# Block-sparse attention and an MLP on one core: the weight loads are released at other points, and the order of all instructions is another one

## The chip, the cores and the metric

The kernel runs on one core of a Trainium2 chip. The metric is the device time of one execution, in microseconds (us). A time is the median of several executions; the profile is of one execution, taken by itself.

The engines are named as the profile names them: PE (TensorE, matmuls; PEld is its weight load), DVE (VectorE), ACT (ScalarE), POOL (GpSimd) and SP (SyncE, which here only issues DMAs). A queue of DMAs is filled by the engine that issues them: SP fills one, POOL another.

## The reference

```
# q, k, v: [4 batches, 8 heads, 768, 64]; w_in: [512, 2048]; w_out: [2048, 512]; all float32
k_rep = k.reshape(B, H, 12, 64, D).mean(axis=3)              # mean key of each block of 64
gate_scores = einsum('bhsd,bhnd->bhsn', q, k_rep)            # causal blocks only
top_idx = argsort(gate_scores)[..., -3:]                     # 3 best blocks of each query
mask = (own block or one of the 3) and (key not after query)
attn = softmax(where(mask, q @ k^T / 8, -1e9)) @ v
x = attn as 3072 tokens x 512
h = x @ w_in
g = 0.5 * h * (1 + tanh(sqrt(2/pi) * (h + 0.044715 h^3)))
out = g @ w_out                                              # [3072, 512] float32
```

## The kernel before

**Tiling.** The 32 heads are worked in 16 pairs (0 to 15), four pairs to a batch of 768 tokens. For a pair the kernel loads q, k and v, turns q and k so that the 64 dimensions of each head lie on partitions, forms the block means of k (`ks`) and their gate scores (the gate, PE), picks the blocks on DVE (`sel`: a transpose, ten rows of MAX8, comparisons), adds the mask through PE, takes the exp on ACT (`ats`), cuts the causal triangle on POOL (affine select), multiplies by v on PE, and normalises and turns the result into `xT`. Batch 0 (pairs 0 to 3) is done by `heads2` with turns on PE; later pairs by `heads`, with turns by DVE's stream transpose (L564) from pieces of 32 partitions in `sd` (four DMAs each for q and for k, L400).

After a batch's four pairs stands its MLP: `s1` (x @ w_in, L1122; gelu on ACT, L1134) and `s2` (the product with w_out). Batch 0 uses a plain second stage (`s2_plain`, L1322, of which f = 0 to 7 need the first half of w_out and f = 8 to 15 the second); batches 1 to 3 use a scheme with fewer products that needs sums of G and of w_out (L1309, L1291) and joins on DVE (L1421). Batch 3's first stage has fewer products too (`s1_seven`, L1211).

**Order.** Each piece of work is an operation that is added to a plan with its engines, what it depends on and which buffers it takes. It is not the program's text that sets the order: a list `ORDER` of operation numbers, with `BUFFER` (which buffer each takes) and `ENGINE` (for operations that may run on several engines, which one), is written out by hand at the top, and `Plan.run` emits the operations in that order. Costs and due times in the `add` calls served the search that made the list. Each engine works through its own instructions in the order in which they were emitted; an instruction that waits holds up what is behind it on that engine. PE also gets "warm" matmuls (L1524) on data of zeros, whose results nobody reads.

**Loads around the change.** Batch 0's q, k, v come through SP, and part of pair 0 through ACT's queue (L428), into room that G and TS need only later. `load_w` issues each weight as two halves from POOL (L460; w_in by columns, w_out by rows of the hidden dimension), and the DMA casts them to float16. In front of w_in stands a small POOL copy (L458) that reads a piece of v of pair 3, so that w_in starts after that v has landed; w_out follows w_in on POOL. `hold` (L1567) is a small DMA on SP that reads the last columns of w_in and so waits for its second half; behind it on SP stand k, q and v of pair 4, and so on. `fill` (L520) puts constant rows into kT. `cast_v` casts v on POOL.

Of the kernel before, what the change touches and what calls it, by code (L numbers as in the profile page):

```python
# [189 lines left out]
    "POOL": [  # L190
        586, 587, 646, 647, 707, 972, 973, 1035, 1036, 1097, 1098,
        1159, 1160, 1425, 1489, 1551, 1612]}


class Op:
# [1431 lines left out]
```

## Time and the profile before

| | us |
|---|---|
| median of 3 runs | 257.90 (257.89 to 257.94) |
| the profiled execution: its span | 256.0 |
| PE busy | 246.5 |
| DVE busy | 191.4 |
| ACT busy | 176.4 |
| POOL busy | 84.3 |
| first matmul with w_in, start | 38.45 |
| w_in issued, first half | 26.97 |
| w_out issued, first half | 34.74 |
| SP's hold lets go | 41.60 |
| last join on DVE, start | 252.70 |

The span is what the profiler's first and last instruction enclose; the time of a run is longer by some 1.9 us, which lie around it. In rows of the timeline the first two numbers are the start and the time of a group of instructions that follow each other on one engine; "x4" counts them, and a bracket gives idle time before them and what ended it. In rows of groups the numbers behind the bar are busy time and the mean of one instruction in nanoseconds.

### The profile page before, as it was taken

The page shows a single profiled execution, that of the slowest core. Times are in us where ns is not written, and L with a number is a line of the kernel's source. Part 1 is how long each engine was busy: PE and PEld are TensorE (multiplying, and loading weights), DVE is VectorE, ACT ScalarE, POOL GpSimd, SP SyncE. Part 2 cuts the span into 40 slices and gives each one's busy share as a digit, 9 for nine tenths or more (in the row PEclk, how much of TensorE's full clock was granted, in tenths as well). Part 3 has the DMA queues.
Part 4 walks back from the last instruction along what each step waited for, and adds up shares of the span by engine and source line. Part 5 has one row for each costly group of instructions (what it writes and reads, how often), then busy time and mean ns, then how long its engine had stood idle before and what let it go on. Part 6 is the DMA issues. An engine that isn't in the chain of part 4 may idle for free.

```text
span 256.0 us, 6451 instructions
## 1 busy us (share of the span) xinstructions
PE 246.5 (96%) x2485; PEld 171.2 (67%) x2485; DVE 191.4 (75%) x539; ACT 176.4 (69%) x225; POOL 84.3 (33%) x163
## 2 busy tenths in 40 slices
PE   7889999999998999999899999999999999999994
PEld 5667686555554566555578888555777786766883
DVE  2769751041989889989999999699889665579954
ACT  2399997634898998667969884566889957557300
POOL 8465970000239366223053853100056620000000
PEclk9999999999999999999999999999999999999999
DMA  8997599999989995999899699532112520040024
GB/s 164 218 208 166 94 212 191 213 161 157 184 142 165 153 143 99 172 179 199 127 174 110 144 188 166 118 94 69 26 34 72 64 74 1 3 165 0 3 82 164
DMA packets 130927, 32.62 MB, mean 127 GB/s; under 512 B 124528, under 2 KB 126928, under 8 KB 130896
## 3 DMA queue, kind: packets, MB, share of 16 engines
q1 hardware_dynamic: 126160, 27.62, 65.4%
q0 software_dynamic: 3136, 4.19, 9.7%
q10 hardware_dynamic: 1600, 0.39, 0.8%
q8 instruction: 19, 0.31, 0.5%
q14 instruction: 12, 0.10, 0.1%
HBM read 27.26 MB, written 6.29 MB: 131 GB/s over the span
## 4 chain that ended last, share of the span: by engine, by line
PE 51%; DVE 16%; SPq 11%; DMA 10%; POOL 4%; issue 3%; ACT 3%; ACTq 1%; DVEq 0%; POOLq 0%
PE bank L1372 17%; PE wide L1122 10%; SPq L400 9%; PE wide L1046 6%; PE wide L1211 5%; DMA w_in<-in_moe_w_in_dram 5%; PE bank L1085 5%; PE bank L1322 3%; DVE qT L367 3%; DMA sd<-in_k_dram 3%; DVE sel L719 2%; DVE s L564 2%; DVE XS L1309 2%; DMA G<-in_q_dram 2%; ACT ats L882 1%
## 5 line engine op out<-in xcount | busy, mean ns | idle before, releaser
L1122 PE MATMUL wide<-xT,w_in 128*128 128x384 f16 x416 | 72.6, 326 | 0.0
L1059 ACT ACTIVATE ats<-wide 128x896 f16<-128x896 f32 x72 | 63.4, 915 | 8.9 <-PE wide L1046 6.2
L1134 ACT ACTIVATE G<-wide 128x768 f16<-128x768 f32 x52 | 42.1, 810 | 27.3 <-PE wide L1122 27.0
L1122 PEld LDWEIGHTS <-w_in 128*128 128x128 f16 x416 | 40.0, 98 | 26.8 <-issue 1.3
L1073 POOL TENSOR_SCALAR_AFFINE_SELECT ats<-ats 128x256 f16<-128x256 f16 x72 | 33.3, 475 | 60.3 <-ACT ats L1059 60.2
L1046 PE MATMUL wide<-qT,kT 76*128 76x512 f16 (+3 forms) x192 | 39.1, 305 | 0.1
L564 DVE STREAM_TRANSPOSE s<-sd 128x768 f32<-128x768 f32 x24 | 23.1, 968 | 18.7 <-DMA sd<-in_k_dram 17.2
L1372 PE MATMUL bank<-w_out,G 128*128 128x256 f16 x216 | 31.4, 272 | 0.0
L1372 PEld LDWEIGHTS <-G 128*128 128x128 f16 x288 | 26.9, 98 | 6.0 <-issue 0.3
L1322 PE MATMUL bank<-w_out,G 128*128 128x512 f16 x96 | 28.1, 379 | 0.0
L365 POOL CAST kT<-s 64x768 f16<-64x768 f32 x17 | 15.2, 891 | 37.5 <-DVE s L564 37.0
L1421 DVE TENSOR_TENSOR osb<-bank,osb 128x512 f32<-128x512 f32 (+1 forms) x38 | 22.1, 592 | 5.1 <-PE bank L1372 4.5
L1085 PEld LDWEIGHTS <-ats 128*128 128x128 f16 x504 | 22.2, 98 | 3.9 <-POOL ats L1073 0.4
L1085 PE MATMUL bank<-v,ats 128*128 128x65 f16 x504 | 24.4, 194 | 0.2 <-POOL ats L1073 0.2
L1046 PEld LDWEIGHTS <-kT 76*128 76x128 f16 x192 | 17.3, 98 | 10.5 <-issue 0.8
L1372 PEld LDWEIGHTS <-XS 128*128 128x128 f16 x216 | 20.0, 98 | 5.5 <-DVE XS L1309 1.5
L1372 PE MATMUL bank<-TS,XS 128*128 128x256 f16 x144 | 22.0, 272 | 0.8 <-DVE XS L1309 0.7
L882 ACT ACTIVATE ats<-wide 128x1024 f16<-128x1024 f32 (+3 forms) x24 | 20.8, 924 | 1.3 <-PE wide L863 0.8
L365 POOL CAST v<-vsd 128x768 f16<-128x768 f32 x13 | 11.4, 875 | 13.8 <-DMA vsd<-in_v_dram 8.8
L969 DVE TENSOR_TENSOR xn<-bank,zr 128x384 f16<-128x384 f32 x24 | 13.4, 558 | 0.8
L719 DVE MAX8 sel<-sel 128x8 f32<-128x12 f32 x160 | 13.2, 158 | 0.6
L1322 PEld LDWEIGHTS <-G 128*128 128x128 f16 x96 | 8.9, 98 | 6.1 <-issue 0.3
(120 smaller groups left out, 358.6 us busy)
## 6 DMA issues: line engine op xcount, KB each, us to landing
out_dram<-osb SPq DMA_DIRECT2D x23, 256.0 KB
vsd<-in_v_dram SPq DMA_DIRECT2D x26, 192.0 KB
sd<-in_k_dram SPq DMA_DIRECT2D x48, 96.0 KB
sd<-in_q_dram SPq DMA_DIRECT2D x48, 96.0 KB
w_in<-in_moe_w_in_dram POOLq DMA_DIRECT2D x2, 1024.0 KB, 11.5
w_out<-in_moe_w_out_dram POOLq DMA_DIRECT2D x2, 1024.0 KB, 14.5
G<-in_k_dram SPq DMA_DIRECT2D x4, 192.0 KB
G<-in_q_dram SPq DMA_DIRECT2D x4, 192.0 KB
```

Source lines behind the costliest of these rows:

```text
L365: nc.gpsimd.tensor_copy(out=out, in_=in_)
L400: nc.sync.dma_start(out=T[key, p][64 * hh + 32 * a:64 * hh + 32 * a + 32], in_=SRC[key][b, 2 * hp + hh].rearrange("(t i) (a j) -> a i t j" ...
L564: nc.vector.transpose(out=T[key + "T32", p], in_=T[key, p].rearrange("p t j -> p (t j)"))
L882: nc.scalar.activation(out=T["at", u][:, :, 0:n], in_=plan.buf[("st",) + u].rearrange("p (h w) -> p h w", h=2)[:, :, 0:n], func=AF.Exp, bi ...
L1046: nc.tensor.matmul(st[:, x:e], kT16[i][h][0:76, s0:s0 + 128], qT16[i][h][0:76, s0 + (x - cb):s0 + (e - cb)], start=True, stop=True)
L1059: nc.scalar.activation(out=T["at", u][:, 0:n], in_=plan.buf[("st",) + u][:, 0:n], func=AF.Exp, bias=0.0, scale=SCALE)
L1073: nc.gpsimd.affine_select(out=dg, in_=dg, compare_op=ALU.is_ge, fill=0.0, base=0, pattern=[[0, 2], [1, 128]], channel_multiplier=-1)
L1085: nc.tensor.matmul(pvv[:, qc, 0:65], at[:, cb + (qc - jc) * 128: cb + (qc - jc + 1) * 128], v16[i][:, jc, h, :], start=(gi == 0 and jc == ...
L1122: nc.tensor.matmul(hps[:, 512 * e:512 * e + HALF], w_in16[:, ci, (2 * j + e) * 128: (2 * j + e + 1) * 128], T["xT", b][:, ci, HALF * h:HAL ...
L1134: nc.scalar.activation(out=G[:, :, h, j, :], in_=plan.buf["hps", b, j, h].rearrange("p (e w) -> p e w", e=2)[:, :, 0:HALF], func=AF.Gelu_a ...
L1322: nc.tensor.matmul(plan.buf["ops", b, ti], G[:, f % 2, 2 * ti // NC, f // 2, ti % (NC // 2) * 128:ti % (NC // 2) * 128 + 128], w_out16[:, ...
L1372: nc.tensor.matmul(dst[:, HD * h:HD * h + HD], FACT[m][0][:, j, t * 128:(t + 1) * 128], FACT[m][1][:, j, :], start=(clear and j == 0), sto ...
```

## The change

1. `load_w` now puts the waiting copy on POOL in front of both weights.
2. w_in waits for v of pair 2 (and, in the plan, for the issue of v of pair 3 on SP) in place of the landing of v of pair 3.
3. w_out is loaded after k and q of pair 4: its copy reads a piece of q of pair 4 and so waits until that has landed. The `hold` stays on SP ahead of k of pair 4.
4. `ORDER`, `BUFFER` and `ENGINE` are other lists. The matmuls are the same but for the warm ones, 63 in place of 39: 54 of them stand before the first product with w_in, formerly 24.

What follows from the new lists, read from the order on each engine:

- SP: a piece of q of pair 1 comes before k of pair 0, and batch 0's later pieces come in another order; behind the hold k, q of pair 4, then v of 4 with one piece of k of 7 between, k of 5, q of 5, then pieces of pairs 6 and 7 mixed.
- ACT issues the second half of q of pair 0 before the first.
- POOL: w_in stands after the first triangle select of pair 1, ahead of that pair's second select and of the casts of v of pairs 1 and 2; w_out stands after the fourth select of pair 3, ahead of the casts of k of pair 4 (both halves are POOL's now) and of v of pair 4.
- ACT has four casts and copies of q and k fewer between its first and its last exp of batch 0; DVE has them. Of later casts some go from DVE to ACT and some back; five casts of k (both of pair 4, one each of pairs 7, 12 and 15) go from DVE to POOL.
- PE: 96 of the 128 products of batch 0 with w_in come before the first product with w_out (72 before), and the gate of pair 4 does too. Between that and the first product that needs w_out's second half stand 22 products with w_in and 8 with w_out.
- The end: PE's last products are those of m7 of the second token group of batch 3, whose join is a whole row of 512, followed by a store of 256 KB; before, the end was a join of half a row and stores of 128 KB.

```diff
@@ lists at the top
 ORDER = [
...
 BUFFER = [
...
 ENGINE = {
...
@@ load_w
         def emit(_):
             x = const.tile([128, 16], FP32, name=f"after_{name}")[96:97]
-            if name == "in":
-                nc.gpsimd.tensor_copy(out=x, in_=T[after][96:97, 0, 1, 0:16])
+            src = T[after]
+            nc.gpsimd.tensor_copy(
+                out=x, in_=src[96:97, 0, 1, 0:16] if len(src.shape) == 4 else
+                src[96:97, 0, 0:16])
             for part in parts:
                 nc.gpsimd.dma_start(out=dst[part], in_=view[part])
@@ main loop
-    for x in ('in', 'out', ('k', HP + 0), ('q', HP + 0), ('v', HP + 0), ('k', HP + 1), ('q', HP + 1), ('v', HP + 1)):
+    for x in ('in', ('k', HP), ('q', HP), 'out', ('v', HP), ('k', HP + 1), ('q', HP + 1), ('v', HP + 1)):
         if x in weights:
             dst, src, parts, prio = weights[x]
             if not fills:
                 fills = [fill(i, chain) for i in range(NB)]
-            load_w(x, dst, src, parts, [ld[prev]] if x == "in" else
-                   [after_w["in", 0]], prio, prev)
+            load_w(x, dst, src, parts, [ld["v", 2], *chain] if x == "in"
+                   else [ld[prev], after_w["in", 0]], prio, ("v", 2) if x == "in" else prev)
             moved_w = [after_w[x]]
             chain += moved_w
```

More of the change, by code (lines that the diff above doesn't have):

```diff
@@ L21 @@
 ORDER = [
[134 rows of a table removed]
-BUFFER = [
[24 rows of a table removed]
[130 rows of a table added]
+BUFFER = [
[24 rows of a table added]
 ENGINE = {
     "ACT": [
[5 rows of a table removed]
[4 rows of a table added]
     "POOL": [
-        586, 587, 646, 647, 707, 972, 973, 1035, 1036, 1097, 1098,
-        1159, 1160, 1425, 1489, 1551, 1612]}
+        337, 338, 586, 587, 646, 647, 707, 708, 972, 973, 1035, 1036, 1097,
+        1098, 1159, 1160, 1425, 1426, 1489, 1551, 1612, 1613]}
 class Op:
```

321 rows, old and new, of tables (BUFFER, ENGINE, ORDER) are left out of this document.

## The prediction

> **What bounds the kernel now.** I read the page first (span, busy shares, slices, chain), then PE in windows, then the stretch from 12 to 66 us on each queue that the change touches.
>
> ```profile
> span 256.0 us, 6451 instructions
> PE 246.5 (96%) x2485; PEld 171.2 (67%) x2485; DVE 191.4 (75%) x539; ACT 176.4 (69%) x225; POOL 84.3 (33%) x163
> DMA  8997599999989995999899699532112520040024
> PE 51%; DVE 16%; SPq 11%; DMA 10%; POOL 4%; issue 3%; ACT 3%; ACTq 1%; DVEq 0%; POOLq 0%
> ```
> ```profile
> 0.00:38.40 38.40, 34.61 (x526) 1.00 1.00 177
> 38.40:50.30 11.90, 11.90 (x82) 1.00 1.28 201
> 66.00:102.00 36.00, 34.77 (x380) 1.00 0.97 141
> 102.00:138.00 36.00, 35.07 (x292) 1.00 1.18 169
> 138.00:256.00 118.00, 114.42 (x1120) 1.00 0.40 81
> ```
>
> The second view is PE by stage: length, busy time, matmuls, granted clock, DMA share, GB/s. PE is full almost everywhere; its idle time is 3.8 us before 38.4, 1.2 us from 66 to 102, 0.9 us from 102 to 138, and 3.6 us after, most of it the tail behind the last matmul. So the kernel is a line of matmuls, and a change gains or loses only where PE waits. The median, 257.9 us, lies 1.9 us above this execution's span; I sum against the span and add 1.9.
>
> Before 38.4 the pace is ACT's. Its rows from 12 us on, an exp, a cast, and the last exps:
>
> ```profile
> 12.50 1.03 ACT L882 ACTIVATE ats<-wide 128x1024 f16<-128x1024 f32 x1
> 13.42 0.49 ACT L363 COPY s<-bank 128x384 f32<-128x384 f32 x1
> 34.82 3.26 ACT L882 ACTIVATE ats<-wide 128x1024 f16<-128x1024 f32 x4 [0.43 <-POOL ats L908]
> L882 ACT ACTIVATE ats<-wide 128x1024 f16<-128x1024 f32 (+3 forms) x24 | 20.8, 924 | 1.3 <-PE wide L863 0.8 <-POOL ats L908 0.4
> ```
>
> The exps fill 20.8 of the 25.6 us from 12.50 to 38.08, and casts most of the rest. The weights come in beside this:
>
> ```profile
> 24.99 0.99 POOL L908 TENSOR_SCALAR_AFFINE_SELECT ats<-ats 128x512 f16<-128x512 f16 x2 [0.93 <-ACT ats L882]
> 25.94 0.83 POOL L365 CAST v<-TS 128x768 f16<-128x768 f32 x1
> 26.97 1.66 POOL L460 DMA_DIRECT2D w_in<-in_moe_w_in_dram  x2
> 34.74 1.78 POOL L460 DMA_DIRECT2D w_out<-in_moe_w_out_dram  x2
> ```
> ```profile
> L460 POOL DMA_DIRECT2D w_in<-in_moe_w_in_dram x2: 747/832/917, 27.0 to 27.9; - x2
> DMA to landing us min/median/max: 9.4/11.5/13.7
> ...
> L460 POOL DMA_DIRECT2D w_out<-in_moe_w_out_dram x2: 881/892/904, 34.7 to 35.6; - x2
> DMA to landing us min/median/max: 12.2/14.5/16.8
> ```
>
> So w_in's halves land 9.4 and 13.7 us after their issues, at 36.4 and 41.6; w_out's at 46.9 and 52.4. PE and SP around it:
>
> ```profile
> 38.45 1.79 PE L1122 MATMUL wide<-xT,w_in 128*128 128x384 f16 x10
> 40.24 10.24 PE L1122 MATMUL wide<-xT,w_in 128*128 128x384 f16 x62
> 50.31 0.38 PE L1322 MATMUL bank<-w_out,G 128*128 128x512 f16 x1
> 56.27 0.71 PE L1524 MATMUL bank<-XS 128*128 128x256 f16 x5
> 59.30 1.24 PE L1322 MATMUL bank<-w_out,G 128*128 128x512 f16 x5
> ```
> ```profile
> 41.60 0.58 SPq L1567 DMA_DIRECT2D after_in<-w_in  x1
> 42.22 7.13 SPq L400 DMA_DIRECT2D sd<-in_k_dram  x4
> 49.40 4.83 SPq L400 DMA_DIRECT2D sd<-in_q_dram  x4
> 55.43 3.07 SPq L400 DMA_DIRECT2D sd<-in_k_dram  x4
> 58.55 2.66 SPq L400 DMA_DIRECT2D sd<-in_q_dram  x4
> ```
>
> The first x@w_in matmul at 38.45 waits for neither weight. SP holds until w_in's second half is there (41.60); then k and q of pair 4 crawl beside w_out, 7.13 and 4.83 us for four pieces where later ones take 3.07 and 2.66.
>
> ```profile
> 54.40 0.98 DVE L564 STREAM_TRANSPOSE s<-sd 128x768 f32<-128x768 f32 x1 [14.96 <-DMA sd<-in_k_dram]
> 57.34 0.98 DVE L564 STREAM_TRANSPOSE s<-sd 128x768 f32<-128x768 f32 x1 [0.18 <-DMA sd<-in_q_dram]
> 63.94 0.35 DVE L703 STREAM_TRANSPOSE sel<-bank 128x160 f32<-128x160 f32 x1 [5.19 <-PE bank L687]
> PE bank L756 <- DVE madd L724: 2.1, 2, 1.2
> PE bank L1372 <- DVE XS L1309: 0.7, 1, 0.7
> ```
>
> DVE is idle for 15 us until k of pair 4, then for 5.2 us more; after that it is packed, and PE waits for it: 2.1 us at masks (the page's stalls near 81 and earlier) and 0.7 us at the sums of batch 1's second stage.
>
> **The change part by part.**
>
> *Start.* SP and ACT issue pair 0's and pair 1's first pieces in another order, with a piece of q of pair 1 ahead of k of pair 0. That should put the first exp about a microsecond later than 12.50. Against it, ACT issues four casts fewer between its first exp and its last (4 x 0.49 = 2.0 us); DVE makes them instead, ahead of the same exps. The exps themselves (20.8 us) do not change. I leave the end of the stretch where it was: 0, with 1.5 us either way. A gain here would also be eaten below, where PE waits for w_out, whose time does not hang on PE. Thirty more warm matmuls stand here. At 0.71 us for five they are 4.3 us of PE time, in a stretch where ACT decides; ACT's exps cover them, and if they did not, the cost would be up to that. After it there are six fewer, in waits that PE has anyway.
>
> *w_in.* Its issue now follows the first triangle select of pair 1 on POOL, one pair's v earlier, instead of the cast of v of pair 2. On ACT eight exps and two casts lead to it: 13.6 + 8 x 0.92 + 2 x 0.49 = 22.0, half of 0.99 for the select, and 1.4 for waits such as the exps' 1.3: 23.9. The bounds are 22.5, without waits, and 25, where before's selects stood. So w_in is issued 3 us earlier and has landed at 33.3 and 38.5. PE gains nothing by that: the first L1122 started 2 us after the first half had landed. Queued behind the wait on POOL are one select and the casts of v of pairs 1 and 2 (about 0.5 and 0.83 each); the two DMA issues (1.66) push them by under 2 us, and ACT's exps cover that. Without the cover it is 1.7 us at most.
>
> *k and q of pair 4, then w_out.* The hold on SP is over at 38.5, k is issued by 39.1 + 3.1 = 42.2 and q by 44.9, now with nothing beside them. Landing comes 2 to 3.1 us later (57.34 less the end of issue at 54.23 is 3.1): 46.9 to 48.0. POOL's copy waits for that piece, so w_out is issued at about 47.2, 12.5 us later than 34.74. Queued behind that wait on POOL are the casts of both halves of k of pair 4 and its v; they are wanted by scores that PE reaches about 15 us later, so they cost nothing here.
>
> The second half of w_out lands between 13.7 us (w_in's way, little beside it) and 16.8 us (its own, eight small pieces beside it) after 47.2: 61 to 64. I take 62, nearer the first, because pair 4's loads are out of the way; v of pair 4 and k of pair 5 are not. The first half lands at about 56.7 to 59.5, by 9.4 and 12.2.
>
> When does PE want them? Before, 72 matmuls with w_in (10 + 62) preceded the first with w_out; now 96 do. 24 more at 10.24 / 62 = 0.165 are 4.0 us, and with the gate of pair 4 now before it, PE stands at the first L1322 at 54.5. The first that needs the second half comes 22 matmuls with w_in and 8 with w_out later (22 x 0.165 + 8 x 0.22, from 1.24 for five): 59.9. Against 62 that is a wait of 2.1 us. Before, five warm matmuls stood in that place, 0.55 us (56.27 to 56.81). Net +1.5; from +0.5 (w_out at 61) to +3.5 (at 64).
>
> *Pairs 4 to 7.* Pair 4's transposes start about 10 us earlier on DVE, in its idle 14.96 us, and its gate comes before the first L1322. The masks of pairs 5 to 7 are still each a chain on DVE (transpose of the gate as in the row at 63.94, ten maxima, mask), and PE's order leaves about as much other work between a gate and its mask as before. Of the 2.1 us of mask waits I let 0.9 go, since PE also arrives later by the wait above; bounds 0 and 2.1. Net -0.9. Where DVE is not late here it is late at its next packed place, the sums below.
>
> *Batch 1's sums.* After the first stretch DVE carries about three copies fewer, moved to POOL and ACT; of the 0.7 us wait for XS I let 0.3 go (bounds 0 and 0.7).
>
> *The end.* Before, the last join is half a row and three 128 KB stores follow each other; now the last product is one of token 1, with a full-row join and a 256 KB store behind it:
>
> ```profile
> 252.70 0.42 DVE L1421 TENSOR_TENSOR osb<-bank,osb 128x256 f32<-128x256 f32 x1 [0.18 <-PE bank L1372]
> L1421 DVE TENSOR_TENSOR osb<-bank,osb 128x512 f32<-128x512 f32 x8 | 5.4, 689 | 1.4 <-PE bank L1372 1.2
> 251.41 2.08 SPq L1465 DMA_DIRECT2D out_dram<-osb  x3
> ```
>
> 0.69 - 0.42 = 0.27 for the join; for the store 0 to 0.5 (twice the bytes; 128 KB at the 201 GB/s of the second window is 0.65 us). I take +0.5 together.
>
> *Sum:* 0 + 1.5 - 0.9 - 0.3 + 0.5 = +0.8: a span of 256.8, and with 1.9 a time of 258.7.
>
> *A rule beside the row.* The Trainium skill, "DMA: Bandwidth & Descriptors", section "Anatomy of one DMA — SWDGE (gpsimd) path", gives 2.0 us plus the bytes over 436 GB/s for a transfer from this engine; as an estimate by that page both halves of w_out (2.1 MB) would be there 6.8 us after the issue. Here the trace differs: 13.7 us for the second half of w_in. By the rule w_out would be there at 54.0, PE would not wait for it, and the sum would be 257.2 or less, which is the first rival's side.
>
> **The rivals.**
>
> *Faster.* w_out comes in time. It needs the w_in issue at 22.5 and w_out in 13.7 us: then everything is 1.4 us earlier than I reckoned, and the second half lands at 47.2 - 1.4 + 13.7 = 59.5, before 59.9. PE loses nothing there, and the 0.55 of warm matmuls go; DVE, 10 us ahead with pair 4, lets the mask waits (2.1) fall to a half, and a wait of 0.7 at XS goes. 257.9 - 0.55 - 1.05 - 0.7 + 0.5 = 256.1, and 255.3 if the first stretch ends 0.8 sooner too. For it: DVE's 15 idle us and SP's 7.13. Against it: w_out 12 us later.
>
> *Slower still.* w_out competes with the small pieces of v of pair 4, k and q of pair 5, as it did with pair 4's, and takes 16.8 us or more. It decides from a landing after 62. Landing at 64 gives a wait of 4.1; nothing of the masks' time is won since pair 5's loads crawl too: 257.9 + 3.5 - 0.9 + 0.5 = 261.0.
>
> *Nothing happens.* The gap in the loads is only moved, from before w_in to before w_out, and PE's wait with it: +0.5 at w_out, -0.9 at masks, +0.4 at the end, 257.9. For it: the same matmuls in all but 24 warm ones; against it, that each of these three terms must fall at one end of its bounds.
>
> **How the numbers follow.** Forecast 0.37 (its own range 258.3 to 259.8); faster 0.33; slower still 0.17; nothing 0.13. The range holds all but about a fifth: 255.8, which leaves out the best ends of the first rival, to 261.0. About 0.5 us, 0.2%, is what a measurement of this kernel can tell from no change. Faster by more than that 0.34, within it 0.13, slower 0.53.
>
> **What would show it.** In the changed kernel: w_in issued near 23.9 and SP's hold over near 38.5; k and q of pair 4 in about 3 us each; w_out issued near 47; PE idle before an L1322 row between 54 and 62, released by DMA of w_out, some 2 us; mask waits at L756's counterpart of 1 to 1.5 us in place of 2.1; the last DVE row 0.69. It is wrong if the first x@w_in matmul moves by over a microsecond, if w_out lands within 12.5 us, or if PE waits for the masks as before or longer.

## The result, and the profile after

| | before | changed |
|---|---|---|
| median of 5 runs | 257.90 us (257.79 to 258.56) | 261.64 us (259.64 to 262.43) |
| ratio, 95% interval | | 1.013 (1.0105 to 1.0155) |
| the profiled execution: its time | | 262.43 us |
| its span | 256.0 | 260.7 |

The change makes the kernel slower by 1.3%. Slower was forecast, at 258.7 us; the median lies 2.9 us above that and 0.6 us above the range. The times of the changed kernel also spread over 2.8 us. Six more runs of it, beside an experiment below, gave a median of 260.13 us (259.38 to 261.59), ratio 1.0103 (1.0079 to 1.0128). In all eleven the times lie between 259.4 and 260.8, or between 261.6 and 262.4. The profile on this page is of the slowest of them; a second profile, of an execution of 259.95 us, is set beside it.

First the page of the changed kernel: span, busy times, the chain that ended last.

```profile
span 260.7 us, 6499 instructions
PE 250.5 (96%) x2509; PEld 174.1 (67%) x2509; DVE 193.4 (74%) x537; ACT 177.2 (68%) x222; POOL 88.2 (34%) x169
PE 66%; DMA 15%; DVE 8%; issue 3%; POOL 3%; ACT 2%; SPq 2%; ACTq 0%; POOLq 0%; DVEq 0%
```

PE is as full as before, and its share of the chain has gone from 51% to 66%. DVE fell from 16% to 8%, the SP queue from 11% to 2%, and DMA rose from 10% to 15%: what was late by DVE and SP now comes late by loads. The waits of PE say which (total, times, longest):

```profile
PE bank L1319 <- DMA w_out<-in_moe_w_out_dram: 2.0, 2, 1.4
PE bank L753 <- DVE madd L721: 1.9, 3, 1.0
PE bank L1369 <- DVE XS L1306: 0.2, 1, 0.2
```

The wait for w_out is new. The sums wait 0.2 us in place of 0.7. The masks wait 1.9 in place of 2.1, but these totals mix two places. In the kernel before, 0.90 us stand in the first stretch, ahead of pair 0's mask (at 9.71), and 1.20 later; in the changed kernel 0.96 and 0.54 stand in the first stretch, and only 0.39 later. The later masks, first before and then after the change:

```profile
81.74 0.45 PE L756 MATMUL bank<-ident,madd 128*128 128x128 f16 x5 [1.20 <-DVE madd L724]
```
```profile
96.18 0.45 PE L753 MATMUL bank<-ident,madd 128*128 128x128 f16 x5 [0.39 <-DVE madd L721]
```

The steps that led to the wait for w_out, on POOL, SP and PE of the changed kernel (start, time):

```profile
25.95 1.66 POOL L457 DMA_DIRECT2D w_in<-in_moe_w_in_dram  x2
...
48.93 0.20 POOL L453 COPY after_out<-sd 1x16 f32<-1x16 f32 x1 [7.81 <-DMA sd<-in_q_dram]
49.39 1.78 POOL L457 DMA_DIRECT2D w_out<-in_moe_w_out_dram  x2 [0.26 <-issue]
```
```profile
40.13 0.58 SPq L1564 DMA_DIRECT2D after_in<-w_in  x1
40.75 2.28 SPq L395 DMA_DIRECT2D sd<-in_k_dram  x4
43.07 2.54 SPq L395 DMA_DIRECT2D sd<-in_q_dram  x4
```
```profile
41.27 0.49 PE L1119 MATMUL wide<-xT,w_in 128*128 128x384 f16 x2
...
59.13 0.38 PE L1319 MATMUL bank<-w_out,G 128*128 128x512 f16 x1 [0.59 <-DMA w_out<-in_moe_w_out_dram]
...
65.96 0.38 PE L1319 MATMUL bank<-w_out,G 128*128 128x512 f16 x1 [1.37 <-DMA w_out<-in_moe_w_out_dram]
```

k and q of pair 4 take 2.3 and 2.5 us for four pieces, a little less than the 3.1 and 2.7 of the forecast. But the first product with w_in stands at 41.27 in place of 38.45, and w_in itself was issued only 1.0 us earlier than before. So the first stretch has lost 2.8 us by this mark, and w_out is issued at 49.39, 2.2 us after the time that was reckoned with.

The beginning shows where the two profiled executions part. PE's first rows of the profile above, and then of the second profile of the same kernel:

```profile
1.07 3.59 PE L1521 MATMUL bank<-XS 128*128 128x256 f16 x16 [1.07 <-DVE bmask L287]
5.39 0.88 PE L545 MATMUL bank<-identk,G 128*128 128x128 f32 x3 [0.72 <-DMA G<-in_q_dram]
6.05 1.49 PE L1521 MATMUL bank<-XS 128*128 128x256 f16 x6
...
11.37 0.32 PE L684 MATMUL bank<-s,ksb 128*32 128x64 f32 x8
```
```profile
1.07 3.60 PE L1521 MATMUL bank<-XS 128*128 128x256 f16 x16 [1.07 <-DVE bmask L287]
5.32 0.52 PE L545 MATMUL bank<-identk,G 128*128 128x128 f32 x3 [0.66 <-DMA G<-in_q_dram]
5.67 0.82 PE L1521 MATMUL bank<-XS 128*128 128x256 f16 x6
...
9.43 0.32 PE L684 MATMUL bank<-s,ksb 128*32 128x64 f32 x8
```

In both PE waits some 0.7 us for q of pair 0. In the execution of 262.43 us the six warm matmuls behind the wait take 1.49 us, in that of 259.95 us 0.82. PE works at half pace in the one and at full pace in the other, and pair 0's gate is at 11.37 or at 9.43, where it was at 6.95 before the change. The granted clock of the page is at 9 (full) in that slice for both, so the pace is to be read from the rows. In the second profile the first product with w_in stands at 39.33, w_out is issued at 47.50, and its second half is first used at 63.73.

### The profile page after: what moved, and what is told of

It reads as the page before. It is cut to its first block, busy times and chain, and to the rows that moved or that the text cites. A ratio compares the mean times of both kernels' runs of the same rounds, so it can differ in the third digit from the quotient of the medians.

```text
span 260.7 us, 6499 instructions
## 1 busy us (share of the span) xinstructions
PE 250.5 (96%) x2509; PEld 174.1 (67%) x2509; DVE 193.4 (74%) x537; ACT 177.2 (68%) x222; POOL 88.2 (34%) x169
## 4 chain that ended last, share of the span: by engine, by line
PE 66%; DMA 15%; DVE 8%; issue 3%; POOL 3%; ACT 2%; SPq 2%; ACTq 0%; POOLq 0%; DVEq 0%
PE bank L1369 20%; PE wide L1119 16%; PE wide L1043 8%; DMA w_out<-in_moe_w_out_dram 6%; PE wide L1208 5%; PE bank L1082 5%; DMA w_in<-in_moe_w_in_dram 5%; PE bank L1319 5%; SPq L395 2%; DMA G<-in_q_dram 2%; PE bank L684 1%; ACT ats L1056 1%; DMA sd<-in_q_dram 1%; DVE sel L716 1%; DVE XS L1306 1%
## 5 line engine op out<-in xcount | busy, mean ns | idle before, releaser
L1119 PE MATMUL wide<-xT,w_in 128*128 128x384 f16 x416 | 73.5, 326 | 0.0
L1056 ACT ACTIVATE ats<-wide 128x896 f16<-128x896 f32 x72 | 62.6, 914 | 6.9 <-PE wide L1043 2.2
L1070 POOL TENSOR_SCALAR_AFFINE_SELECT ats<-ats 128x256 f16<-128x256 f16 x72 | 32.2, 462 | 51.9 <-ACT ats L1056 51.2
L1369 PE MATMUL bank<-w_out,G 128*128 128x256 f16 x216 | 32.1, 272 | 0.0
L1369 PEld LDWEIGHTS <-G 128*128 128x128 f16 x288 | 27.3, 98 | 6.7 <-issue 0.3
L1082 PEld LDWEIGHTS <-ats 128*128 128x128 f16 x504 | 21.2, 98 | 4.7 <-POOL ats L1070 1.1
L1082 PE MATMUL bank<-v,ats 128*128 128x65 f16 x504 | 23.5, 194 | 0.1
L1369 PE MATMUL bank<-TS,XS 128*128 128x256 f16 x144 | 22.8, 272 | 0.2 <-DVE XS L1306 0.2
L360 POOL CAST kT<-s 64x768 f16<-64x768 f32 x22 | 19.0, 865 | 5.8 <-DVE s L561 5.0
L1521 PE MATMUL bank<-XS 128*128 128x256 f16 x63 | 14.8, 327 | 1.1 <-DVE bmask L287 1.1
## 6 DMA issues: line engine op xcount, KB each, us to landing
out_dram<-osb SPq DMA_DIRECT2D x23, 256.0 KB
```

The costliest lines, as they stand in the source:

```text
L360: nc.gpsimd.tensor_copy(out=out, in_=in_)
L1056: nc.scalar.activation(out=T["at", u][:, 0:n], in_=plan.buf[("st",) + u][:, 0:n], func=AF.Exp, bias=0.0, scale=SCALE)
L1070: nc.gpsimd.affine_select(out=dg, in_=dg, compare_op=ALU.is_ge, fill=0.0, base=0, pattern=[[0, 2], [1, 128]], channel_multiplier=-1)
L1082: nc.tensor.matmul(pvv[:, qc, 0:65], at[:, cb + (qc - jc) * 128: cb + (qc - jc + 1) * 128], v16[i][:, jc, h, :], start=(gi == 0 and jc == ...
L1119: nc.tensor.matmul(hps[:, 512 * e:512 * e + HALF], w_in16[:, ci, (2 * j + e) * 128: (2 * j + e + 1) * 128], T["xT", b][:, ci, HALF * h:HAL ...
L1369: nc.tensor.matmul(dst[:, HD * h:HD * h + HD], FACT[m][0][:, j, t * 128:(t + 1) * 128], FACT[m][1][:, j, :], start=(clear and j == 0), sto ...
```

## The experiments

The kernels are made from the changed one or from the one before by moving instructions in the written order; none leaves out any of the computation. "First stretch" is batch 0's attention with its loads. All medians are of four runs or more beside runs of the kernel before on the same chip, whose medians were 257.61 to 257.78 for e1 to e16; the ratios are to these. The last three columns are of each one's profile, in us. The first product with w_in is not quite the same mark everywhere: in the kernels with the changed rest 18 to 26 products with v, some 0.8 us of PE's time, stand behind it that stand ahead of it, all or nearly all, in before, e4, e5, e8 and e10.

```
kernel                          median  ratio (95% interval)       first with  w_out   second half
                                                                   w_in        issued  first used
before                          257.90                              38.45      34.74   56.81
changed                         261.64  1.0130 (1.0105 to 1.0155)   41.27      49.39   65.96
changed, again                  260.13  1.0103 (1.0079 to 1.0128)   39.33      47.50   63.73
e1  first stretch of before     260.78  1.0116 (1.0090 to 1.0143)   38.24      47.83   65.01
e2  w_out early                 267.60  1.0360 (1.0320 to 1.0401)   39.56      34.34   70.91
e3  e1 and e2                   265.05  1.0289 (1.0266 to 1.0312)   38.23      31.08   68.59
e4  before + new first stretch  260.44  1.0106 (1.0080 to 1.0132)   42.22      39.02   60.73
e5  before + w_out late         269.69  1.0469 (1.0452 to 1.0485)   38.48      49.92   68.49
e6  PE's first gap filled       259.67  1.0090 (1.0066 to 1.0115)   39.65      47.70   63.66
e7  e1, no loads beside w_out   261.05  1.0140 (1.0124 to 1.0156)   38.27      47.22   62.55
e8  before + w_in early         257.88  1.0013 (1.0004 to 1.0021)   38.82      35.11   57.18
e9  pair 0's start of before    262.63  1.0194 (1.0173 to 1.0214)   40.41      48.67   65.53
e10 before + e9's stretch       261.40  1.0166 (1.0122 to 1.0210)   44.63      41.43   63.13
e11 q of pair 1 behind k of 0   259.69  1.0078 (1.0062 to 1.0094)   39.69      47.64   63.80
e13 e11, w_out behind k of 4    258.14  1.0023 (1.0012 to 1.0035)   39.51      44.79   61.92
e14 e1, wait filled             260.03  1.0087 (1.0073 to 1.0100)   38.24      47.59   63.94
e15 e1, w_out behind k of 4     258.07  1.0020 (1.0006 to 1.0033)   38.23      44.61   61.53
e16 e15, first piece of k       268.58  1.0401 (1.0378 to 1.0424)   38.24      42.20   72.09
```

**Is it the start, or w_out?** Theory A took the new first stretch for the cause, theory B w_out's lateness. Four kernels.

```diff
 e1: changed kernel
-first stretch: changed order, buffers, engines
+first stretch: those of the kernel before; w_in behind a select of pair 0 on POOL
```


> The changed kernel with the first stretch (all of batch 0's attention on every engine, its loads and its warm matmuls) in the order, buffers and engines of the kernel before; w_in is still released by v of pair 2 and stands on POOL after the third-last select of pair 0; the rest is the changed kernel's. Theory A, the new order of the first stretch is what costs: first x@w_in matmul near 38.5 in place of 41.3, w_in issued near 24, hold over near 38.5, w_out issued near 47; PE then waits 3 to 4 us for w_out; time 258.3 to 259.7. Theory B, the loss is w_out's lateness and what follows it: the time stays above 261, since w_out's landing sets the middle whatever the start does.


```diff
 e2: changed kernel
-POOL: ..., last select of pair 3, copy that waits for q of pair 4, w_out
+POOL: ..., cast of v of pair 3, w_out
```


> The changed kernel with w_out issued on POOL right after the cast of v of pair 3, without its waiting copy, as before the change; the start is the changed one. Theory A: the 2.0 us that PE waited for w_out go, some of it comes back at pair 4's gate and masks, because k and q of pair 4 crawl beside w_out again; time 259.5 to 261. Theory B: time 258 or less.

e3 has both edits.

> Both at once: first stretch of the kernel before, w_out early, the rest of the changed kernel. Theory A: the two add up, 256.5 to 258.2. Theory B: no better than the run with w_out early alone, by over 0.5 us.


```diff
 e4: kernel before
-first stretch, w_in released by v of pair 3
+first stretch of the changed kernel, w_in released by v of pair 2
```


> The kernel before with only the first stretch in the changed kernel's order, buffers and engines, its warm matmuls and w_in released by v of pair 2; w_out and all that follows as before the change. Theory A: first x@w_in matmul 2.5 to 3 us later than 38.45, time 260 to 261.5. Theory B: first x@w_in matmul the same within 1 us or its lateness made up for later, time within 0.7 of 257.9.

e4 came out as theory A said: the new first stretch alone costs 2.5 to 2.8 us (ratio 1.0106), though w_out is early in it. But e1 did not. Its start is right again (38.24), and yet the time is 260.78, within the two medians of the changed kernel: w_out is issued at 47.83, no earlier than in the second profile of the changed kernel (47.50), and PE, which comes sooner, waits 2.4 us for it in place of 1.7. Both theories have half of it. The two losses lie side by side on the way to the same product, and the later one sets the time; undoing the start alone wins nothing.

e2 is over 6 us above both expectations, and e3 as far above theory A's; e3 is 2.5 us below e2, so the start counts there too. What PE waits for in e2:

```profile
PE bank L694 <- DVE s L571: 6.4, 1, 6.4
```

The changed order has pair 4's gate on PE ahead of the first product with w_out. With w_out early, k and q of pair 4 come beside it (SP's rows there: 9.96 and 4.37 us for four pieces), DVE turns them late, and PE stands 6.4 us at the gate. So the late w_out is no slip that can be taken out alone: the order needs k and q of pair 4 first.

**What each half does to the kernel before.**

```diff
 e5: kernel before
+            else:
+                nc.gpsimd.tensor_copy(out=x, in_=T["q", 4][96:97, 0, 0:16])
-POOL: ..., select of pair 3, w_out, two selects of pair 3, ...
+POOL: ..., three selects of pair 3, w_out, ...
```


> The kernel before with w_out alone moved: issued on POOL after the last select of pair 3, behind a copy that waits for q of pair 4; k and q of pair 4 right behind the hold as before; nothing else. Theory A2, w_out's lateness costs by itself and the changed order of PE (24 more products ahead of it) takes back about half: w_out issued near 50, second half there near 66.5, where PE asks for it at 56.8; time 263 to 267. Rival: the later masks had slack enough to take it, time under 261.


```diff
 e8: kernel before
-                nc.gpsimd.tensor_copy(out=x, in_=T[after][96:97, 0, 1, 0:16])
+                nc.gpsimd.tensor_copy(out=x, in_=T["v", 2][96:97, 0, 1, 0:16])
-POOL: ..., cast of v of pair 2, w_in
+POOL: ..., select of pair 0, w_in
```


> The kernel before with w_in alone released by v of pair 2, on POOL after the third-last select of pair 0; w_out and all else as before. Expected: w_in issued near 24.2 (26.97), hold over near 38.7 (41.6), first x@w_in matmul the same; k and q of pair 4 2 to 3 us earlier at DVE, mask waits fall by 0.5 to 1.5 us; time 256.3 to 257.4, the useful half of the change. Rival: the hold's 3 us only move k and q of pair 4 deeper under w_out; 257.5 to 258.2.

With w_out late and nothing else, the kernel takes 269.69 us, more than was expected; PE waits 9.2 us for it, and the granted clock is at 0.50 behind the wait until about 64. The rest of the change, as e1 has it, is worth some 9 us against that (269.69 less 260.78): 24 more products ahead of w_out, the rest of the new order, and w_in's earlier release, by which w_out is issued at 47.83 in place of 49.92. In the kernel before that release, the part that looked useful, does nothing: 257.88 beside 257.65 is within the 0.2% that counts as no change, and the first product with w_in comes 0.4 us later (38.82). SP and PE in e8:

```profile
38.72 0.58 SPq L1571 DMA_DIRECT2D after_in<-w_in  x1
39.34 9.58 SPq L404 DMA_DIRECT2D sd<-in_k_dram  x4
48.97 5.38 SPq L404 DMA_DIRECT2D sd<-in_q_dram  x4
```

The hold lets go 2.9 us earlier, and k of pair 4 takes 9.58 us in place of 7.13 under w_out. q's issue ends at 54.35, where it ended at 54.23, and the masks wait 2.0 us, nearly as long as before. That was the rival written with it.

**PE's pace.** The two profiles of the changed kernel suggested theory C, that PE's wait of 0.7 us at the start decides its pace behind it.

```diff
 e6: changed kernel
 PE: 16 warm matmuls,
+    4 more warm matmuls,
     turn of q of pair 0
```


> The changed kernel with four more warm matmuls on PE ahead of the first turn of q of pair 0, which fill the 0.7 us in which PE waits for that load (4.66 to 5.39). Theory C, that gap leaves PE at half pace (warm matmuls 0.24 us apart) until 10 us in some executions and not in others: now all executions have full pace from 5.5 us on, gate of pair 0 near 9.7, times within 1 us of each other, 259.3 to 260.3. Rival: the pace has nothing to do with the gap; times spread over 259.6 to 262.4 as before.

Four of the six times lie between 258.81 and 259.88, but two are 260.59 and 261.31. The median is 0.5 us below that of the changed kernel's second set, inside the intervals. The expectation failed as to the spread. It failed as to the pace too: in e6's profile PE does not wait for q any more, and is at half pace all the same when it comes to that turn. So it is in e13, an experiment below, where the wait there is 0.22 us. PE's rows of e6, then of e13:

```profile
1.07 4.45 PE L1534 MATMUL bank<-XS 128*128 128x256 f16 x20 [1.07 <-DVE bmask L300]
5.43 0.87 PE L558 MATMUL bank<-identk,G 128*128 128x128 f32 x3
6.09 1.17 PE L1534 MATMUL bank<-XS 128*128 128x256 f16 x6
```
```profile
4.88 0.88 PE L557 MATMUL bank<-identk,G 128*128 128x128 f32 x3 [0.22 <-POOL G L507]
5.55 1.49 PE L1533 MATMUL bank<-XS 128*128 128x256 f16 x6
```

So the wait does not bring the half pace. PE has it from its first matmul on in every profile (e6's 20 warm ones take 4.45 us, the 16 of the changed kernel 3.59, so one takes 0.21; later six take 0.82 and five 0.71, so one takes 0.11), and what differs is when it ends: by 5.3 us in the second profile of the changed kernel, and at about 6.8 in e6, 6.9 in e13, 9.2 in e4 and 10.2 in the first profile. With the start of the kernel before it ends between about 4.4 and 6.6, and costs nothing: pair 0's mask stands at 9.70 to 9.72 in all eleven profiles with that start. The new order has twice as many turns ahead of the first gate, 12 of k and 12 of q where before there were 6 and 6, and there a late end makes the gate late. Whether the wait makes the half pace last longer stays open. The two latest ends come behind a wait of 0.7 to 0.9 us, but so do two of the early ones, those of the second profile and of e2.

The changed kernel again:

> The changed kernel once more, for the spread of its times and one more profile. Theory C (PE's pace at the start differs from one execution to the next): if this profile's time is under 260.3, its first turns run at full pace (six warm matmuls in about 0.8 us) and the gate of pair 0 is near 9.7; if it is over 261, half pace (1.5 us) and the gate after 11. Rival: no such pairing, or gates alike in both.

Its profile was of an execution of 259.95 us, and it has the full pace and the gate at 9.43, as shown above: the pairing holds. It rests on two profiles of this kernel. e4's first rows agree on the half pace (its six warm matmuls take 1.49 us in an execution of 260.93, where its six times go from 259.47 to 261.73).

```diff
 e11: changed kernel
-SP: q of pair 1 (first piece), k of pair 0, ...
+SP: k of pair 0, q of pair 1 (first piece), ...
```


> The changed kernel with one thing moved on SP: the first piece of q of pair 1 is issued behind k of pair 0 in place of ahead of it. If that piece is what makes pair 0 late, gate of pair 0 near 9 and the time 0.5 to 1.5 below the changed kernel's. If it is PE's order (both turns of q of pair 1 ahead of the gates) or PE's slow pace, the gate stays at 9.7 or later and the time the same within 0.5.

The gate stays at 9.79: ahead of it PE now waits 1.0 us for another load of q (at 8.91), so moving that piece alone does not bring pair 0 forward. The times are all between 258.98 and 260.14: PE comes to its first turn at 4.84, after a wait of 0.18 us, and is at full pace by 5.3 in the profile. That looked like support for theory C, but e13 has the same beginning, and half pace until 6.9.

A wait in the middle of the kernel is another matter. e1 waits for w_out. Its times were 259.56 to 260.43 in three executions and 261.12 to 261.83 in three, and the mean granted clock 0.998 to 1.0 in the first three, 0.992 to 0.993 in the others. PE in windows, in the profile of 261.5 us (start and end, length, busy, granted clock, DMA share, GB/s):

```profile
56.00:58.00 2.00, 0.00 (x0) 1.00 1.27 175
58.00:60.00 2.00, 1.97 (x10) 0.80 1.38 201
60.00:62.00 2.00, 2.00 (x8) 0.50 1.44 218
62.00:64.00 2.00, 2.00 (x11) 0.85 1.22 186
64.00:66.00 2.00, 2.00 (x13) 1.00 0.86 129
```
```profile
58.03 0.38 PE L1328 MATMUL bank<-w_out,G 128*128 128x512 f16 x1 [2.41 <-DMA w_out<-in_moe_w_out_dram]
...
59.66 3.25 PE L1128 MATMUL wide<-xT,w_in 128*128 128x384 f16 x10
```

The clock falls about a microsecond after the wait of 2.41 us has ended and is at a half for some 3 us, and ten products take 3.25 us that took 1.79 before the change. So the wait costs a second time. Longer waits did so every time: behind the 6.0 to 9.2 us of e2, e3, e5 and e16 the mean clock was 0.981 to 0.987 in all 20 executions.

```diff
 e14: e1
 PE: ..., products of batch 0 with w_in,
+    22 warm matmuls,
     first product with w_out
```


> The run with the old first stretch (e1_start), with 22 warm matmuls (2.4 us at full pace) on PE ahead of the first product with w_out, where it waits 2.4 us for w_out. Theory F, that wait lets the granted clock fall to a half for some 3 us in part of the executions (mean clock 0.992 to 0.993, 261.1 to 261.8, beside 0.998 to 1.0, 259.6 to 260.4): now the clock is 0.998 or more in all, times within 259.4 to 260.6. Rival: the low clock and the spread stay.

All four times lie between 259.36 and 260.11, at a clock of 0.998 or more. This one closed the spread as expected. Theory F is borne out for this wait, though four executions against three low ones of six are few. The Trainium skill's page "TensorE: Matmul & The Clock Gate", section "Part 1: The HAM clock gate (the "warmup" mystery)", says that PE's clock is halved after an idle window of about 3.4 us, and that the window runs on its own, so that the moment at which the pace changes varies. The rows agree with the half (0.50), and the six executions with a part of chance. They do not agree with the length: here a wait of 2.41 us was enough, shown in one profile and, by the mean clock, in two more executions of the six.

**What makes w_out late.**

```diff
 e7: e1
+            if (key, p) == ("v", 4):
+                nc.sync.dma_start(out=after_in[0:1],
+                                  in_=w_out16[0:1, NF - 1, DM - 16:DM])
```


> The run with the old first stretch (e1_start), and a second small DMA on SP that reads the last row of w_out ahead of v of pair 4, so that nothing else is loaded while w_out comes. Theory D, the small pieces beside it delay w_out: its second half is there 11 to 13.5 us after its issue in place of 15.4, PE waits 2 to 4 us less there, later gates are in time all the same; time 257.5 to 259.5. Rival: w_out takes 15 us whatever is beside it, or pairs 5 to 7 come too late: 260.5 or more.

How long w_out's two halves are under way, from the issue of each to its landing, first in e7, where every other load is held back, then in e1:

```profile
DMA to landing us min/median/max: 10.0/12.1/14.1
```
```profile
DMA to landing us min/median/max: 10.2/12.8/15.4
```

Alone on the queues the second half takes 14.1 us, beside the small pieces 15.4 (14.9 to 18.3 in all the profiles with loads beside it). Theory D expected 11 to 13.5. The half is first used at 62.55 in place of 65.01, but the time did not fall (261.05): the pieces held back are missing later, where PE waits 0.5 us at XS, 0.4 us for a turn and 0.3 us for a cast of v. So most of the 15.4 us is w_out's own, and what is left to move is its issue.

```diff
 e13: e11
-            src = T[after]
+            src = T[after if name == "in" else ("k", HP)]
```


> The run with q of pair 1 behind k of pair 0 on SP (e11_q1_behind), and w_out released by k of pair 4 in place of q of pair 4. Theory E, w_out's landing sets the time from 57 us on, and each microsecond of its issue comes back there until PE's own arrival decides: w_out issued 2 to 2.5 us earlier (near 45.3), first use of its second half 1.2 to 2 us earlier than 63.8, time 257.8 to 258.7. Rival, the wait only moves to pair 4's gate and masks, or w_out comes slower beside q of pair 4: 259.2 or more.

w_out is released by k of pair 4 and issued 2.9 us earlier than in e11 (47.64). POOL's row in e13, and what PE waits for:

```profile
44.79 1.78 POOL L469 DMA_DIRECT2D w_out<-in_moe_w_out_dram  x2 [0.26 <-issue]
```
```profile
PE bank L1533 <- DVE bmask L299: 1.1, 1, 1.1
PE bank L765 <- DVE madd L733: 1.7, 3, 0.8
PE bank L557 <- POOL G L507: 0.2, 1, 0.2
```

The wait for w_out is gone, its second half is first used 1.9 us earlier than in e11, and the time falls by 1.55 us, to 258.14 (one of the twelve executions took 261.62, at a mean clock of 0.993). Theory E is borne out: w_out's release by q of pair 4, undone alone, gives back most of what e11 had lost, with the start still the changed one.

e15 has this release and the old first stretch.

> The run with the old first stretch (e1_start), and w_out released by k of pair 4 in place of q of pair 4: both losses undone at once. w_out issued near 44.8, second half there near 61.5, PE asks for it near 60.3. Theory E: time 257.0 to 257.9, 0.3 to 1.1 below the run with the changed start and the same release (258.1). Rival: no lower than that run.

258.07 us, no lower than e13 by more than can be told, so the expected 257.0 to 257.9 was missed by a little. With both losses undone the kernel is back at the one before (1.002, 1.0006 to 1.0033), and no version was found that beats it. PE still waits 0.4 us for w_out there. e16 tried a still earlier release:

```diff
 e16: e15, w_out's copy reads another partition of k of pair 4
-                src[96:97, 0, 0:16])
+                src[0:1, 0, 0:16])
```


> The same, with w_out released by the first piece of k of pair 4 in place of its last. If w_out still is late in e15, another 1 to 2 us of its issue come back: 256.5 to 257.5. Rival, q of pair 4 is then loaded beside w_out and comes late for pair 4's gate, at which PE's order waits before the first product with w_out: 258.5 or more.

```profile
PE bank L694 <- DVE s L571: 8.5, 1, 8.5
```
```profile
57.10 0.98 DVE L571 STREAM_TRANSPOSE s<-sd 128x768 f32<-128x768 f32 x1 [10.14 <-DMA sd<-in_q_dram]
```

The rival came, much larger than written: 268.58 us, with 8.5 us of waiting at pair 4's gate for q. In e15 SP has issued all of q (by 43.8) when w_out's issue begins at 44.61; in e16 w_out, at 42.20, comes in the middle of that (41.69 to 43.94). Between the two issues lies a step of 10 us.

**Two that told little.** e9 and e10 put pair 0's beginning of the kernel before in front of the changed rest of the first stretch.

```diff
 e9: changed kernel; e10: the same first stretch in the kernel before
-pair 0 up to its first exp: changed order
+pair 0 up to its first exp: order of the kernel before
```


> The changed kernel with only pair 0's beginning, up to its first exp, as in the kernel before (loads of k and q of pair 0 first, its gates ahead of pair 1's turns, the warm matmuls of that stretch); all later work of the first stretch and the rest as changed. Theory A: first exp back at 12.5, first x@w_in matmul back near 38 or up to a microsecond earlier (ACT's four casts fewer), but PE then waits 4 to 5 us for w_out, so the time is only 0.5 to 1.5 below the changed kernel's: 260 to 261.2. Theory B, the loss of the first stretch sits in its later part: first x@w_in matmul after 40.

> The kernel before with the first stretch of e9_first_pair (pair 0's beginning as before, the later part and w_in's release as changed), and w_out and all that follows as before. Theory A: no worse than the kernel before, 256.8 to 258.2, since neither of the two losses is in it. Theory B: 259 or more.

In e9 the gate is at 7.04 again, but PE then waits 2.3 us for loads of q, and the first product with w_in comes at 40.41. e10 is 3.8 us slower than the kernel before, and its times fall apart: 260.37 to 260.50 in three executions with a mean clock of 0.998 to 0.999, 262.31 to 263.76 in three with 0.987 to 0.993. In the profile, of the second kind, PE waits 0.8 and 1.8 us between 13.8 and 16.8, and the granted clock is 0.50 from 17 to 22. At full clock e10 is still 2.8 us above the kernel before. The loads' order and PE's order of a first stretch fit each other, and the mixture fits neither. This speaks for theory B of that pair (the later part of the stretch loses too), but since the mixture has waits of its own it does not say how much.

## Why the prediction was wrong, point by point

*Where the miss sits.* The sum has the second half of w_out first used at 62. It was used at 63.73 in the second profile, at 65.96 in the first, and at 63.94 in e14, which has the start that the prediction assumed and no slow clock behind the wait: 1.7, 4.0 and 1.9 us late. The forecast of +0.8, this lateness, and the small corrections of the other terms below (-0.3, -0.1 and -0.3) make +2.2, +4.7 and +2.4, and the three spans are just that much above the 256.0 of before. So two steps failed: the landing of w_out was mis-sized, and the start was put at nothing.

*k and q of pair 4, then w_out.* As a mechanism this step was right. The hold (predicted 38.5) lets go at 38.54 in the second profile, k and q take 2.3 us each, and w_out is issued at 47.50 (47.2). The landing was too early: "I take 62" is 14.8 us after the issue of the first half. The second half is issued 0.9 us after the first, which the same prediction had reckoned for w_in and left out here, and takes 15.3 us from its own issue: 47.50 + 0.9 + 15.3 = 63.7. It takes hardly less alone (14.1). The wait for the first half is left out of the sum as well, though by the prediction's own figures (PE there at 54.5, landing at 56.7 to 59.5) it is 2.2 to 5.0 us. In e1 it is the only wait for w_out: PE stands at the first product at 55.62 (58.03 - 2.41), a microsecond after the 54.5, since 18 products with v now stand behind the first product with w_in.

*Start: "0, with 1.5 us either way".* This step failed. The first exp at 13.6 was right at full pace (13.55). But "ACT issues four casts fewer (2.0 us)" did not make up for it:

```profile
33.80 5.19 ACT L879 ACTIVATE ats<-wide 128x1024 f16<-128x1024 f32 x6 [0.62 <-PE wide L860]
39.00 1.28 ACT L826 ACT_TABLE_LOAD   x1
```
```profile
L879 ACT ACTIVATE ats<-wide 128x1024 f16<-128x1024 f32 (+3 forms) x24 | 20.7, 916 | 2.2 <-PE wide L860 1.8
```

These are ACT's last exps in the second profile, and all its exps of batch 0. The last end at 39.0, 0.9 us later than before the change. Ahead of its 24 exps ACT now waits 2.2 us, 1.8 of them for scores from PE, where it waited 1.3 and 0.8. In the first profile, with the long half pace, the first product is 2.8 us late. Alone, with the rest as before, this stretch costs 2.7 us (e4).

*"A gain here would also be eaten below, where PE waits for w_out, whose time does not hang on PE."* The first half of this sentence was right (e1), the second was not. w_in follows a select, which follows an exp, which follows PE's turns. The long half pace moves w_in from 24.01 to 25.95, and by way of hold, k and q it moves w_out from 47.50 to 49.39 and its first use from 63.73 to 65.96. This chain is 2.2 of the 2.5 us by which the one profiled execution lies above the other.

*PE's pace.* Not in the prediction at all. It was argued there that warm matmuls are covered. That PE begins at half pace, that the end of it varies, and that the new order hangs on it, was left out; so was the clock behind a long wait. That the start's pace makes the spread of the changed kernel's times rests on its two profiles and one of e4; what makes the half pace end early or late stays open.

*Pairs 4 to 7, sums and the end.* The -0.9 for the later masks came out at -0.8 (1.20 to 0.39). It was reckoned from 2.1 us, of which 0.90 was pair 0's wait at 9.71 and not of these pairs at all, so that the size is in part luck; and "PE waits for the masks as before" was a poor sign, since the total hides the gain behind longer waits in the first stretch. The sums' wait fell by 0.5 in the first profile, and in the second and in e14 the list of waits has it no more (0.3 was let go). The end is as reckoned: from the last join to the end of the span there were 256.0 - 252.70 = 3.3 us, and now 260.7 - 256.86 = 3.8, +0.5.

*The rivals.* "Slower still" came near with 261.0, but in part by luck. A landing at 64 is what happened (63.7 to 65.9); its reason, loads beside w_out, is worth 1.3 us (e7), and most of the lateness was w_out's own time and its issue. Its sum leaves the start at nothing and takes off 0.9 for masks that its own words say are not won; without that it is 261.9. "Faster" needed w_out in 13.7 us. By the rule in the Trainium skill, "DMA: Bandwidth & Descriptors", section "Anatomy of one DMA — SWDGE (gpsimd) path", the estimate was 6.8, and no run came near that: 14.1 us with nothing beside it.

## What to carry to other kernels

When two loads are put in another order, work out the landing of the one that goes last from its own issue and with the slowest row seen, and ask what its release hangs on, back to the first instruction: a weight that waits for a small load that waits for a hold that waits for an exp inherits every delay of the start. Two lost stretches on the way to one product need not add up: here undoing the start alone won nothing that can be told, undoing the late release alone 1.6 us, and both together no more than that. So undo each alone and both before you judge either. And fill a wait of some 2 us on PE, if it can't be removed: PE may pay for it twice.

## What was not expected of the hardware

A wait of 2.41 us on PE was followed by a granted clock of 0.50 for about 3 us in e1's profile, and the mean clock was as low (0.992 to 0.993) in three executions of six; with warm matmuls in the wait it was low in none of four. Waits of 6.0 to 9.2 us brought it in 20 executions of 20. At the start PE was at half pace from its first matmul (0.21 us for a warm matmul in place of 0.11) while the granted clock of the page stood at full; this ended anywhere between about 4.4 and 10.2 us. Four pieces of k took SP 2.3 us with nothing beside them and 7 to 11 us beside a weight (7.13 before, 9.58 in e8, 11.00 in e13), and the second half of w_out felt them much less: 14.9 to 18.3 us in place of 14.1.
